# The order of two sums at the end of the first column: the half in the score banks ahead of the half in the value banks

## The chip, the cores and the metric

One core of one Trainium2 chip. The metric is the device time of one execution in microseconds, over several runs of each kernel. The changed kernel and the kernel before take turns on the same chip.

## The reference, cut to what matters

A gated attention unit feeds a gated feed-forward layer. Eight batches of 3008 rows, width 256, key width 64, hidden width 2048; inputs and output are float32.

```python
scores = scale * np.matmul(z, z.transpose(0, 2, 1))
attn = np.maximum(scores, 0.0) ** 2
out = np.matmul(attn, v)
attn_out = u * out
# ... as [24064, 256] = x into
h = x @ w_in
g = h * np.cos(h)
return (g @ w_out).astype(np.float32)
```

## The kernel before, where the change touches it

The attention is worked column by column (512 columns of the score matrix at a time). In the first three columns `phase_a_first` puts the value matmuls of both output halves beside the next scores. Each half takes two accumulators, one for the upper 64 rows and one for the lower 64, so four banks for a column: M0 and M1, and a pair E taken out of the rotation of three score pairs. A half is summed when the column ends:

```python
def gate_sum(s, b0, b1):
    W = width(s % NC)
    sm = spool.tile([P, CW], FP32, name="sm")
    nc.scalar.copy(sm[:, 0:W], b0[:, 0:W])
    nc.vector.tensor_tensor(sm[:, 0:W], b1[:, 0:W], sm[:, 0:W], ALU.add)
    return sm

def hold(src):
    nc.gpsimd.tensor_copy(mark[:, 0:1], src)

def phase_a_first(s, n, extra={}):
    # ...
    pair = [E[ea][:, 0, :], E[ea][:, 1, :]]
    acc = [pair, M] if s == 1 else [M, pair]
    # ... value matmuls and scores; within the loop, in later columns:
            if dh > 0 and (k % 4 == 3):
                drop_piece((b, J, k // 4))
                if s > 0:
                    emit_turns((0, 0), 1)      # one transpose of a piece A, on the SP queue
                    if k < 4:
                        turn_u(s)              # transpose of u, on the same queue
    # ... at the end of the column:
    late_sums.extend(gate_sum(s, *acc[dh]) for dh in range(2))
    hold(late_sums[0][0:1, 0:1])
    load_u(s + 1)
    e_order.append(ea)
```

`hold` is a one-element GpSimd copy that reads a sum. GpSimd works in order, so the load of the next u behind it isn't issued before that sum exists. The order of the calls:

```python
phase_a_first(0, 12, {4: lambda: turn_late(4), 8: lambda: turn_late(5)})
phase_a_first(1, 12)
nc.gpsimd.dma_start(w_out16, moe_w_out.rearrange("(k p) f -> p k f", p=P))
for i in range(2):
    emit_h(0, i)()
phase_a_first(2, 14)
# ...
phase_b(2)                                     # first use of w_out16
```

## Time and profile before

| | before |
|---|---|
| median of three runs | 1193.32 us (1192.68 to 1193.82) |
| span in the profile | 1191.2 us |
| TensorE busy | 1183.7 us, 99% |
| TensorE waits for the sum L278 | once, 0.7 us |

The lines are in the prediction below. A row of the timeline reads: start, duration, engine, line, operation, output<-inputs, shape, count, and in brackets the idle time ahead of it with what ended it. SPq is the queue of the DMA transposes. A transfer's landing is the moment at which its end is signalled. A row of the waits reads: who waited, for whom, total, times, longest.

On GpSimd, in the timeline of before: the hold and the load of u behind it, and the load of the output weights one column later.

```profile
24.49 0.18 POOL L353 CAST mark<-sm 1x1 f16<-1x1 f32 x1 [9.96 <-DVE sm L278]
24.72 0.57 POOL L148 DMA_DIRECT2D u<-in_u_dram  x1
...
39.09 1.18 POOL L721 DMA_DIRECT2D w_out<-in_moe_w_out_dram  x1
```

### The profile page before, as it was taken

To read this page: it belongs to the slowest core of one execution; us is meant where nothing else is said; L and a number is where in the kernel's file an instruction comes from. 1 tells how busy PE (TensorE), PEld (TensorE's weight loads), DVE (VectorE), ACT (ScalarE), POOL (GpSimd) and SP (SyncE) were. 2 spreads that over 40 slices of the span, in tenths; PEclk is the share of its full clock that TensorE was granted. 3 is DMA by queue.
4 is the path that set the end of the run, shared out by engine and by line. 5 is a ranking of instruction groups with operands and counts; after the bars stand their busy time and mean duration, and the time that the engine had idled before them with its cause. 6 is when DMAs were issued, how large, how long until landed. Compare 5 with 4: busy or idle time off the path is not lost.

```text
span 1191.2 us, 29044 instructions
## 1 busy us (share of the span) xinstructions
PE 1183.7 (99%) x11887; PEld 726.8 (61%) x11887; DVE 1011.5 (85%) x1302; ACT 794.9 (67%) x927; POOL 679.0 (57%) x717
## 2 busy tenths in 40 slices
PE   9999999999999999999999999999999999999998
PEld 4556665665566656666566665656666566665566
DVE  6888888889988898888988889888888888888776
ACT  7966676667666676667676676666766666666454
POOL 3286745657466573755647556476555655545452
PEclk9999999999999999999999999999999999999999
DMA  9999999569995799955999469984798837974301
GB/s 160 175 172 158 115 171 130 102 122 104 173 127 101 123 137 166 126 89 103 155 152 130 86 106 158 168 123 70 120 162 152 122 72 120 173 122 84 65 20 54
DMA packets 449142, 148.00 MB, mean 124 GB/s; under 512 B 401264, under 2 KB 432496, under 8 KB 449008
## 3 DMA queue, kind: packets, MB, share of 16 engines
q1 hardware_dynamic: 368464, 112.93, 56.6%
q0 software_dynamic: 80032, 32.78, 27.7%
q8 instruction: 93, 1.52, 0.5%
q10 hardware_dynamic: 512, 0.43, 0.1%
q14 instruction: 41, 0.34, 0.1%
HBM read 66.32 MB, written 24.64 MB: 76 GB/s over the span
## 4 chain that ended last, share of the span: by engine, by line
PE 98%; ACT 1%; DVE 1%; issue 0%; POOL 0%; DVEq 0%; ACTq 0%
PE E L412 27%; PE M L490 23%; PE M L266 20%; PE E L266 19%; PE E L202 6%; PE M L533 1%; ACT r L212 1%; PE M L468 1%; DVE g L423 0%; PE E L673 0%; DVE sm L278 0%; PE E L533 0%; POOL s L441 0%; PE M L696 0%; ACT c L420 0%
## 5 line engine op out<-in xcount | busy, mean ns | idle before, releaser
L420 ACT ACTIVATE c<-E 128x1024 f16<-128x1024 f32 (+1 forms) x384 | 385.7, 1007 | 216.4 <-PE E L412 214.1
L423 DVE SCALAR_TENSOR_TENSOR g<-E,c 128x1024 f16<-128x1024 f32 (+1 forms) x384 | 458.9, 1197 | 62.0 <-ACT c L420 60.9
L212 ACT ACTIVATE r<-E 128x512 f16<-128x512 f32 (+1 forms) x342 | 328.0, 967 | 112.3 <-PE E L202 106.6
L266 PEld LDWEIGHTS <-v 64*128 64x128 f16 x4512 | 245.7, 94 | 229.6 <-issue 18.8
L412 PE MATMUL E<-x,w_in 128*128 128x512 f16 (+1 forms) x1408 | 354.0, 375 | 0.0
L441 POOL TENSOR_TENSOR s<-g 128x512 f16<-128x512 f16 (+1 forms) x184 | 207.8, 1130 | 189.3 <-DVE g L423 139.4
L266 PE MATMUL M<-A,v 64*128 64x512 f16 (+1 forms) x2256 | 283.0, 372 | 0.0
L266 PE MATMUL E<-A,v 64*128 64x512 f16 (+1 forms) x2256 | 278.0, 371 | 0.0
L442 POOL TENSOR_TENSOR g<-g 128x512 f16<-128x512 f16 (+1 forms) x184 | 219.0, 1190 | 14.4
L412 PEld LDWEIGHTS <-w_in 128*128 128x128 f16 x1536 | 133.1, 98 | 108.9 <-issue 19.5
L490 PEld LDWEIGHTS <-g 128*128 128x128 f16 x2816 | 172.5, 98 | 40.8
L217 DVE TENSOR_TENSOR A<-r 128x1024 f16<-128x1024 f16 x240 | 173.2, 734 | 15.1 <-ACT r L212 14.3
L294 POOL TENSOR_TENSOR x<-sm,uT 128x512 f16<-128x512 f32 (+1 forms) x43 | 48.6, 1131 | 223.5 <-DVE sm L278 223.5
L490 PEld LDWEIGHTS <-s 128*128 128x128 f16 x2112 | 129.4, 98 | 32.1 <-DVE s L448 0.5
L202 PE MATMUL E<-zT 64*128 64x512 f16 (+4 forms) x684 | 128.0, 356 | 1.6 <-DVE sm L278 0.7
L448 DVE TENSOR_TENSOR s<-s,g 128x1024 f16<-128x1024 f16 (+1 forms) x92 | 99.7, 1085 | 2.1 <-POOL s L441 2.1
L490 PE MATMUL M<-w_mix,s 128*128 128x128 f16 x1408 | 94.0, 219 | 0.3 <-POOL s L441 0.3
L490 PE MATMUL M<-w_mix,g 128*128 128x128 f16 x1408 | 93.6, 219 | 0.0
L490 PE MATMUL M<-w_out,g 128*128 128x128 f16 x1408 | 93.6, 219 | 0.0
L220 DVE TENSOR_TENSOR A<-r 128x512 f16<-128x512 f16 (+1 forms) x102 | 80.1, 785 | 8.6 <-ACT r L212 7.6
L202 PEld LDWEIGHTS <-zT 64*128 64x128 f16 x684 | 38.7, 94 | 38.4 <-issue 3.8
L450 DVE TENSOR_TENSOR s<-g,s 128x1024 f16<-128x1024 f16 (+1 forms) x92 | 60.6, 661 | 0.0
(58 smaller groups left out, 636.3 us busy)
## 6 DMA issues: line engine op xcount, KB each, us to landing
out_dram<-o SPq DMA_DIRECT2D x87, 256.0 KB, 2.1
v<-in_v_dram POOLq DMA_DIRECT2D x40, 256.0 KB, 11.5
u<-in_u_dram POOLq DMA_DIRECT2D x40, 256.0 KB, 4.5
A<-A SPq DMA_TRANSPOSE x252, 5.3
z<-in_z_dram POOLq DMA_DIRECT2D x14, 192.0 KB, 10.9
z<-in_z_dram POOLq DMA_DIRECT2D x14, 176.0 KB, 6.8
v<-in_v_dram POOLq DMA_DIRECT2D x8, 192.0 KB, 16.1
u<-in_u_dram POOLq DMA_DIRECT2D x8, 192.0 KB, 3.7
```

Of the source, the lines that this page charges most:

```text
L202: nc.tensor.matmul(e[:, t, 0:Wt], zT[rows, k * P:(k + 1) * P], zT[rows, J * CW:J * CW + Wt], start=True, stop=True,)
L212: nc.scalar.activation(r[:, :, 0:W], e[:, :, 0:W], AF.Relu)
L217: nc.vector.tensor_tensor(a4, r4, r4, ALU.mult)
L220: nc.vector.tensor_tensor(a4, r[:, :, 0:W], r[:, :, 0:W], ALU.mult)
L266: nc.tensor.matmul(bank[:, 0:width(J)], vs[b, k // 4][t * H:(t + 1) * H, k % 4, dh * P:(dh + 1) * P], value_rhs(b, J, k, t), start=start, ...
L412: nc.tensor.matmul(e[:, f, 0:W], w_in16[:, k, ft * P:(ft + 1) * P], x[:, k, 0:W], start=(k == 0), stop=(k == 1),)
L420: nc.scalar.activation(c[:, :, 0:W], e[:, :, 0:W], AF.Sin, bias=half_pi, scale=inv_s2)
L423: return lambda: nc.vector.scalar_tensor_tensor(gs[m][:, 2 * i:2 * i + 2, 0:W], e[:, :, 0:W], 1.0, c[:, :, 0:W], ALU.mult, ALU.mult)
L441: nc.gpsimd.tensor_tensor(s1[:, f, 0:n], g[:, f, low], g[:, lower, low], ALU.add)
L442: nc.gpsimd.tensor_tensor(g[:, f, low], g[:, f, up], g[:, f, low], ALU.subtract)
L448: nc.vector.tensor_tensor(s2[:, f, 0:n], s1[:, f, 0:n], g[:, f, up], ALU.subtract)
L490: nc.tensor.matmul(acc[:, k * P:(k + 1) * P], left[:, ft, k * P:(k + 1) * P], right[:, ft, :], start=(ft == 0 and k == 0), stop=(ft == F - ...
```

## The change

Intent: release the score pair first, since a score needs it before any value matmul needs M.

```diff
         if s == 0:
             turn_u(0)
-        late_sums.extend(gate_sum(s, *acc[dh]) for dh in range(2))
+        sums = {dh: gate_sum(s, *acc[dh]) for dh in ((1, 0) if s == 0 else (0, 1))}
+        late_sums.extend(sums[dh] for dh in range(2))
         hold(late_sums[0][0:1, 0:1])
         load_u(s + 1)
         e_order.append(ea)
```

`hold` still reads the sum of the first half, which is now formed second.

## The prediction

> **What bounds the kernel now.** I read the page first, for the engine that sets the span, then that engine's waits, then the stretch where the longest of them stands. From the page:
>
> ```profile
> span 1191.2 us, 29044 instructions
> PE 1183.7 (99%) x11887; PEld 726.8 (61%) x11887; DVE 1011.5 (85%) x1302; ACT 794.9 (67%) x927; POOL 679.0 (57%) x717
> ...
> PE 98%; ACT 1%; DVE 1%; issue 0%; POOL 0%; DVEq 0%; ACTq 0%
> ```
>
> The TensorE is busy 1183.7 of 1191.2 us and carries 98% of the chain that ended last. All that it does not work is 1191.2 - 1183.7 = 7.5 us, and a change that leaves its matmuls alone can win only from there. Where that idle time lies is said by the waits of the TensorE, complete:
>
> ```profile
> PE E L673 <- DVE s L636: 1.2, 1, 1.2
> PE E L202 <- DVE sm L278: 0.7, 1, 0.7
> PE E L202 <- DVE g L423: 0.4, 1, 0.4
> PE M L490 <- POOL s L441: 0.3, 1, 0.3
> PE E L202 <- ACT zT L666: 0.3, 1, 0.3
> PE E L202 <- DVE zT L668: 0.2, 1, 0.2
> ```
>
> The second row is the one that the change aims at: once in the run, a score matmul (L202, into a pair of score banks E) waits for a sum (L278). The timeline from 22 to 26.5 us shows it:
>
> ```profile
> 22.52 0.38 PE L266 MATMUL M<-A,v 64*128 64x512 f16 x1
> 22.72 0.83 PE L266 MATMUL E<-A,v 64*128 64x512 f16 x6
> 22.99 0.58 ACT L277 COPY sm<-M 128x512 f32<-128x512 f32 x1
> 23.13 0.69 DVE L220 TENSOR_TENSOR A<-r 128x1024 f16<-128x1024 f16 x1 [0.34 <-ACT r L212]
> ...
> 23.46 0.60 ACT L277 COPY sm<-E 128x512 f32<-128x512 f32 x1
> 23.58 0.83 PE L266 MATMUL E<-A,v 64*128 64x512 f16 x6
> 23.74 0.68 DVE L278 TENSOR_TENSOR sm<-M,sm 128x512 f32<-128x512 f32 x1
> ...
> 24.34 0.68 DVE L278 TENSOR_TENSOR sm<-E,sm 128x512 f32<-128x512 f32 x1
> ...
> 25.07 0.39 PE L202 MATMUL E<-zT 64*128 64x512 f16 x2 [0.66 <-DVE sm L278]
> 25.29 0.61 PE L266 MATMUL E<-A,v 64*128 64x512 f16 x4
> 25.50 2.11 ACT L212 ACTIVATE r<-E 128x1024 f16<-128x1024 f32 x2 [0.51 <-PE E L202]
> 25.72 0.61 PE L266 MATMUL M<-A,v 64*128 64x512 f16 x4
> ```
>
> The first column has its first output half in the two banks M0 and M1 and its second half in a pair E. Each half is summed by a ScalarE copy (L277) of one bank and a VectorE addition (L278) of the other. M is summed first, though the E pair is what the next-but-one score needs; the matmul that reuses M comes later in the TensorE's order, at 25.72 us.
>
> **What the Trainium skill says.** "PSUM — Partial Sum Buffer", section on bank collisions, asks for semaphores by bank between engines, so the score may not touch the pair before the addition has read it; here the score starts 25.07 - (24.34 + 0.68) = 0.05 us after the addition's end, which agrees. The same page, "Engine vs sequencer instructions", says that matmuls start in program order; so the ready value matmuls behind the score wait too, and the trace shows none before 25.07. "TensorE: Matmul & The Clock Gate", "Back-to-back issue gap", gives about 216 ns for 512 columns; here 23.37 to 23.58 us from a score pair to the value pair behind it, 0.21, where two 64-row matmuls on different row halves go side by side. "Perfetto Trace Analysis", on the TensorE instruction, says that the ends are estimated; so I count from starts, not from the 0.66.
>
> **The change, part by part.** The order of instructions of both builds was compared. No instruction is added or removed. On ScalarE the two copies swap, on VectorE the two additions swap, the rest keeps its place. Two first matmuls of the second column into M0 and M1 get an explicit wait (for the copy of M0, for the addition of M1). Nothing in the other 1160 us differs.
>
> 1. Copy of E: ScalarE is free for it at 22.99 (it follows the last relu of the column). The pair's last value matmul started with that of M0 at 22.52; results reach ScalarE about 0.43 us after a start (25.07 to 25.50), thus 22.95. It fits by 0.04, so the copy begins at 22.99 and ends near 23.58.
> 2. Addition of E: it takes the place of the first addition, at 23.74, behind the square of 23.13, and ends at 23.74 + 0.68 = 24.42.
> 3. Score: 24.42 + 0.05 = 24.47 in place of 25.07, a gain of 0.60 us. Without any wait it would go three pairs after 23.58, at 23.58 + 3 x 0.216 = 24.23. So the wait is 25.07 - 24.23 = 0.84 now and 0.24 after: the change takes 0.60 of it and leaves 0.24 (0.06 by the profile's way of counting idle time).
> 4. M: its addition now comes second, 24.34 to 25.02, and with 0.05 frees M1 at 25.07. The first value matmul into M stands 25.72 - 25.07 = 0.65 behind the score, so at 24.47 + 0.65 = 25.12. It fits by 0.05 us.
> 5. Behind it: from 25.07 to 36.4 the scores start at steps of 0.86 or 1.08 us, four or five pairs of 0.216, so there the TensorE never waits and ScalarE follows it. ScalarE ends its earlier relu near 24.99 and can take the next from about 24.9, when the score's result is there. So the whole column moves 0.6 us earlier.
> 6. The 0.4 us wait of 39.88 us (score for L423) hangs on the last relu of the second column, its copies, additions and two L423: all follow ScalarE and so the TensorE, and move along. The wait stays 0.4 and eats nothing.
>
> The chain of waits of before confirms that the two additions lie on the path here and the TensorE after them:
>
> ```profile
> 23.13 0.69 DVE A L220
> 23.82 1.21 DVE sm L278 x2
> 25.03 0.04 issue
> 25.07 0.39 PE E L202 x2
> 25.46 0.43 PE E L266 x4
> ```
>
> One addition less on it is 1.21 / 2 = 0.60, the same by a second way. No wait of the TensorE after 45 us is longer than 0.3, so 0.60 us should arrive at the end: 1193.32 - 0.6 = 1192.7 us.
>
> **Rivals.**
> (a) The wait moves to M: the addition that frees M1 ends 0.05 us before it is needed. If signals come 0.1 us later than I take them, the TensorE stops at 25.12 instead for about that long. For it: the margin is as small as what I can read from the timeline. Against: even if M made it wait as long as E did, no more than the 0.60 could go. It would make 1192.8, at worst 1193.3.
> (b) A later load takes it back. The load of the next u is held back until the sum of the first half is formed (a small POOL copy, 24.49), and that sum moves from 24.42 to 25.02. The transpose of this u starts at 29.16 as it lands, and five transposes of A follow it on the same queue to 49.3 us; all may come 0.6 us later while the TensorE comes 0.6 us earlier. Against: the first three columns compute their own score pieces and wait for no transposed piece. The transposed u of this slot is first used at 45.86, some 13 us after its landing; the source pieces are overwritten from 48.9 us on, those of the transposes of 39.03 and before. The output weights, issued at 39.09 and 14.4 us to landing (53.49), are used at 54.62: 1.1 us of slack for load and transposes to push each other about. It would make 1193.0 to 1193.5.
> (c) The wait at 39.88 swallows the gain, if VectorE does not come earlier there. It would make 1193.3. Against: step 6; VectorE's squares before it all wait for ScalarE (0.22 to 0.39 us each).
> (d) The run-to-run spread hides everything: the three runs of before lie between 1192.68 and 1193.82, 1.14 us, twice the effect. This I hold to be certain for single runs; it does not change the middle.
>
> **Range and chances.** The whole idle time of the TensorE is 7.5 us, 0.6% of the time, and 2% would be 23.9 us: faster by over 2% cannot come from this change, and nothing that it moves could cost so much short of a disturbed run. So within 2% gets 0.99. The middle is 1192.7. The gain itself I put between 0 and 0.7 us; with half the spread of the runs on either side the range is 1192.0 to 1193.5.
>
> **What would show it.** Right: the copy of E at 22.99 and its addition at 23.74; the score at 24.47 with hardly any idle before it; in the waits of the TensorE, the 0.7 for the sum gone or 0.1; the first M matmul of the second column near 25.12; the wait of 0.4 still there, near 39.3 us; the TensorE's busy time still 1183.7 and the span near 1190.6; VectorE's idle before its second square of the column falling from 0.84 to about 0.3; the transpose of u at 29.8. Step 1 is wrong if the copy of E starts late, step 4 if a wait of M matmuls (L266) for the sum appears, step 6 if the wait for L423 grows towards 1 us, rival (b) if the TensorE waits for a DMA anywhere. The prediction as a whole is wrong if the same rounds on one chip show the changed kernel slower, or faster by over 1 us.

## The result and the profile after

| | before | after |
|---|---|---|
| median | 1194.12 us (1192.68 to 1197.46, 6 runs) | 1196.70 us (1195.15 to 1197.47, 6 runs) |
| ratio of the fast runs | 1 | 1.0015 (1.0000 to 1.0031) |
| span in the profile | 1191.2 us | 1193.5 us |
| TensorE busy in the profile | 1183.7 us | 1183.3 us |
| TensorE waits for the sum | 0.7 us | none |
| TensorE waits for the output weights | none | 2.9 us |

A ratio is the mean time of one kernel's fast runs over that of the other's in the same rounds, so it isn't quite the ratio of the medians. By the 2% threshold this is "same", but its middle is a loss (the interval just touches 1), and the prediction had a gain of 0.6 us. A second set of rounds (below, the changed kernel again) gave 1.0022, with 1 outside the interval.

The page of after, and the TensorE's waits:

```profile
span 1193.5 us, 29044 instructions
...
PE 1183.3 (99%) x11887; PEld 726.7 (61%) x11887; DVE 1010.9 (85%) x1302; ACT 794.2 (67%) x927; POOL 679.3 (57%) x717
```

```profile
PE M L534 <- DMA w_out<-in_moe_w_out_dram: 2.9, 1, 2.9
PE E L674 <- DVE s L637: 1.2, 1, 1.2
...
PE E L202 <- DVE g L424: 0.4, 1, 0.4
```

The wait for the sum is gone and a new one leads the list. Its size fits the span: 2.90 new less 0.66 removed is 2.24 us, and the span grew by 1193.5 - 1191.2 = 2.3. So nothing else of size happened, and the place to look is one transfer.

The timeline of after around the swapped sums:

```profile
22.75 0.58 ACT L277 COPY sm<-E 128x512 f32<-128x512 f32 x1
...
23.34 0.83 PE L266 MATMUL E<-A,v 64*128 64x512 f16 x6
23.49 0.68 DVE L278 TENSOR_TENSOR sm<-E,sm 128x512 f32<-128x512 f32 x1
...
24.09 0.68 DVE L278 TENSOR_TENSOR sm<-M,sm 128x512 f32<-128x512 f32 x1
24.23 0.39 PE L202 MATMUL E<-zT 64*128 64x512 f16 x2
...
24.78 0.69 DVE L217 TENSOR_TENSOR A<-r 128x1024 f16<-128x1024 f16 x1
24.84 0.68 POOL L353 CAST mark<-sm 1x1 f16<-1x1 f32 x1 [11.34 <-DVE sm L278]
24.87 0.61 PE L266 MATMUL M<-A,v 64*128 64x512 f16 x4
...
25.46 0.57 POOL L148 DMA_DIRECT2D u<-in_u_dram  x1
```

This execution is 0.24 us early as a whole (its value matmuls ahead of the wait start at 23.34, in before at 23.58). With that taken off, the score starts at 24.23 + 0.24 = 24.47, as predicted. The hold's copy is the row to look at: it took 0.68 us in place of 0.18, and the load behind it was issued at 25.46, just as the square of 24.78 ended (24.78 + 0.69 = 25.47). The load of u was issued 25.46 + 0.24 - 24.72 = 0.98 us later than in before, not 0.60.

From the same timeline, one column later, the load of the output weights, VectorE held by a transpose of A, and the TensorE where it lost the time:

```profile
38.24 1.17 POOL L722 DMA_DIRECT2D w_out<-in_moe_w_out_dram  x1
...
52.65 1.29 DVE L217 TENSOR_TENSOR A<-r 128x1024 f16<-128x1024 f16 x2 [1.47 <-DMA A<-A]
...
56.84 1.05 PE L534 MATMUL M<-w_out,g 128*128 128x256 f16 x8 [2.90 <-DMA w_out<-in_moe_w_out_dram]
```

The load was issued 0.85 us earlier than in before (38.24 against 39.09) and landed 3.3 us later. The view of the tile of the output weights gives the time to landing, in before and then in after:

```profile
DMA to landing us min/median/max: 14.4/14.4/14.4
```

```profile
DMA to landing us min/median/max: 18.5/18.5/18.5
```

39.09 + 14.4 = 53.5 us against 38.24 + 18.5 = 56.7 us. What slowed it is on the transposes' queue. Its timeline in before, and then in after (start, duration of the issue, count):

```profile
29.16 1.94 SPq L168 DMA_TRANSPOSE uT<-u  x1
31.19 18.10 SPq L252 DMA_TRANSPOSE A<-A  x5
49.38 4.04 SPq L168 DMA_TRANSPOSE uT<-u  x1
```

```profile
29.33 1.49 SPq L168 DMA_TRANSPOSE uT<-u  x1
30.91 21.64 SPq L252 DMA_TRANSPOSE A<-A  x5
52.65 3.98 SPq L168 DMA_TRANSPOSE uT<-u  x1
```

The five transposes of A took 3.5 us longer too. So both transfers are slower while they run side by side.

### The profile page after: what moved, and what is told of

Its sections match the earlier page's. It is cut to its first block, busy times and chain, and to the rows that moved or that the text cites. A ratio compares the mean times of both kernels' runs of the same rounds, so it can differ in the third digit from the quotient of the medians.

```text
span 1193.5 us, 29044 instructions
## 1 busy us (share of the span) xinstructions
PE 1183.3 (99%) x11887; PEld 726.7 (61%) x11887; DVE 1010.9 (85%) x1302; ACT 794.2 (67%) x927; POOL 679.3 (57%) x717
## 4 chain that ended last, share of the span: by engine, by line
PE 95%; DMA 2%; issue 1%; ACT 1%; DVE 0%; POOL 0%; ACTq 0%; POOLq 0%
PE E L413 27%; PE M L491 23%; PE M L266 20%; PE E L266 18%; PE E L202 5%; DMA w_out<-in_moe_w_out_dram 2%; PE M L534 1%; ACT r L212 1%; PE M L469 1%; PE E L674 0%; PE E L534 0%; DVE g L424 0%; DVE sm L278 0%; POOL s L442 0%; POOL u L148 0%
## 5 line engine op out<-in xcount | busy, mean ns | idle before, releaser
L443 POOL TENSOR_TENSOR g<-g 128x512 f16<-128x512 f16 (+1 forms) x184 | 219.3, 1192 | 14.4
```

Of the source, the lines that this page charges most:

```text
L443: nc.gpsimd.tensor_tensor(g[:, f, low], g[:, f, up], g[:, f, low], ALU.subtract)
```

## The experiments

**The theories.** A: the change itself makes the output weights late each time, by shifting transfers against each other. A1: the later hold alone does it. A2: it takes the later hold and the earlier TensorE together. B: the landing is chance, alike in both kernels. Twelve kernels were run, five rounds each, in three groups of four; the kernel before ran nine times in each group. The second group (runs 5 to 8) ran on another chip than the other two.

**1. The kernel before once more** (no edit).

> The kernel before, unchanged, for a second trace. Theory A (the reordered sum moves the load of the output weights into the transposes, each time): the output weights land ahead of their first use as in the first trace of before, the TensorE waits 0.7 us for the sum and not at all for that load, ratio to before 1.000. Rival B (the load's landing is chance from run to run, in both kernels alike): a wait of 1 to 3 us for the output weights may stand here too, and the 6 timed runs of before, 1192.7 to 1197.5, are this spread.

Measured: 1193.08 us against 1193.16, ratio 0.9999 (0.9987 to 1.0012). The waits are those of the first trace: the sum 0.7, no load. The weights needed 15.8 us from 38.87 and thus landed at 54.7. The TensorE's timeline of this trace, and then of the first one:

```profile
52.66 1.90 PE L412 MATMUL E<-x,w_in 128*128 128x512 f16 x8
54.67 1.05 PE L533 MATMUL M<-w_out,g 128*128 128x256 f16 x8
```

```profile
52.88 1.90 PE L412 MATMUL E<-x,w_in 128*128 128x512 f16 x8
54.62 1.04 PE L533 MATMUL M<-w_out,g 128*128 128x256 f16 x8
```

From the start of the eight matmuls to the first use of the weights it is 2.01 us here and 1.74 in the first trace. So the TensorE did wait 0.27 us for the weights; the list of waits hides it, as it counts from the estimated ends. The kernel before had no slack at all in this execution, where the first trace had shown 1.1 us.

**2. The changed kernel once more** (no edit).

> The changed kernel, unchanged, for a second trace. Theory A: again a wait of 2 to 3.5 us of the TensorE for the output weights, no wait for the sum, ratio 1.0015 to 1.002. Rival B: the wait may be absent or of another length, and the ratio over more rounds falls to 0.9995 to 1.001.

Measured: 1196.29 us (1194.24 to 1197.95) against 1193.16, ratio 1.0022 (1.0009 to 1.0034). Its waits:

```profile
PE M L534 <- DMA w_out<-in_moe_w_out_dram: 1.0, 1, 1.0
...
PE M L534 <- DVE sm L278: 0.3, 1, 0.3
```

The wait is there again. The profiled execution was the quickest of the five (1194.24), which fits 1.0 in place of 2.9. The size falls short of what theory A had said for the trace; the loss over the rounds is just above the 1.0015 to 1.002 that it had said. B is out as the cause of the loss: two sets of rounds show it, and of two traces each the changed kernel has waits of 1.0 and 2.9 us and the kernel before none and 0.27. But the landing does vary from run to run.

**3. The output weights one column earlier, in the changed kernel.**

```diff
+    nc.gpsimd.dma_start(w_out16, moe_w_out.rearrange("(k p) f -> p k f", p=P))
     phase_a_first(1, 12)
-    nc.gpsimd.dma_start(w_out16, moe_w_out.rearrange("(k p) f -> p k f", p=P))
     for i in range(2):
```

> The changed kernel with the load of the output weights issued one column earlier (ahead of the second column, behind the load of the next u) instead of behind the second. Both theories expect the wait for the output weights gone. Theory A: the gain of the reordered sum then shows, TensorE idle 2.3 to 3 us less than in the changed kernel, ratio to before 0.9990 to 0.9998; a small wait may be left, since the sum of the second column on VectorE came late as well, behind a square that waited 1.5 us for a transpose. If the ratio stays at 1.0015, the load was not what cost the time.

Measured: 1192.58 us (1192.28 to 1193.04) against 1193.16, ratio 0.9993 (0.9981 to 1.0006), span 1190.6, no wait for a load and none for the sum. The load of the weights is where the time was lost; without it the span is the 1190.6 us that was predicted, though the interval of the ratio includes 1.

**4. The hold on the sum that is formed first, in the changed kernel.**

```diff
-        hold(late_sums[0][0:1, 0:1])
+        hold(sums[1 if s == 0 else 0][0:1, 0:1])
```

> The changed kernel, but the small GpSimd copy that holds back the next load of u waits for the sum that is now formed first (of the second half), so the load isn't 0.6 us later. Theory A1 (the transposes are late because the load of u and its transpose were held back by the later sum): the transpose queue runs 0.5 to 0.6 us earlier, the wait for the output weights falls under 1 us, ratio 0.9995 to 1.0005. Theory A2 (the load of the output weights starts 0.9 us sooner with the TensorE and so meets a whole transpose that it trailed before): the wait stays at 2 to 3 us, ratio 1.001 to 1.002.

Measured: 1192.57 us (1192.42 to 1193.09) against 1193.16, ratio 0.9994 (0.9980 to 1.0007), span 1190.8. The hold's copy is short again, and the weights, issued only 0.35 us later than in the changed kernel, land in 13.7 us (52.3). From the timeline of this kernel, GpSimd:

```profile
24.49 0.18 POOL L353 CAST mark<-sm 1x1 f16<-1x1 f32 x1 [9.96 <-DVE sm L278]
24.72 0.57 POOL L148 DMA_DIRECT2D u<-in_u_dram  x1
...
38.59 1.18 POOL L722 DMA_DIRECT2D w_out<-in_moe_w_out_dram  x1
```

The theory A2 for this run, that the earlier load of the weights alone is enough, is out: the earlier TensorE alone costs nothing, and in the changed kernel the later hold is necessary for the loss.

**5. The later hold alone, in the kernel before.**

```diff
-        hold(late_sums[0][0:1, 0:1])
+        hold(late_sums[1 if s == 0 else 0][0:1, 0:1])
```

> The kernel before, sums in the old order, but the small GpSimd copy that holds back the next load of u reads the second sum in place of the first; nothing else. Theory A1 (the later hold alone is what costs): the copy stands at about 25.1 us, takes 0.68 instead of 0.18 us behind a VectorE square, the load of u starts about 1.1 us later than in before, the TensorE keeps its 0.7 us wait for the sum and gets a wait of 0.5 to 3 us for the output weights; ratio 1.001 to 1.003. Theory A2 (the reordered additions and the earlier TensorE are needed for the loss): ratio 0.9995 to 1.0005.

Measured: 1193.05 us against 1193.30, ratio 0.9997 (0.9984 to 1.0010), no wait for the weights. The copy was long and the load of u late as expected:

```profile
25.03 0.68 POOL L353 CAST mark<-sm 1x1 f16<-1x1 f32 x1 [11.48 <-DVE sm L278]
25.66 0.57 POOL L148 DMA_DIRECT2D u<-in_u_dram  x1
```

The expectation from A1 failed: a hold that delays the load of u by 0.94 us (25.66 against 24.72) costs nothing by itself either. A2 holds at this delay: it takes both. Run 10 asks what a longer delay does.

**6. The control for 3: the weights one column earlier, in the kernel before.** The edit is that of 3.

> The kernel before with the load of the output weights one column earlier, the control for the same edit of the changed kernel. Theory A1: in before this load was in time, so nothing is won: ratio 0.9995 to 1.0005, and the same edit of the changed kernel (0.9993) is then 0.0005 better by the reordered sum alone. If the ratio here is 0.9993 too, the gain of that run came from the earlier load and not from the sum.

Measured: 1193.01 us (1192.91 to 1193.42) against 1193.30, ratio 0.9994 (0.9980 to 1.0007). It keeps its 0.7 us for the sum and has the span of before, 1191.2. The ratio lies a hair under what was expected, drawn by one run of before at 1197.06; the medians differ by 0.3 us. Its span against that of run 3, 1191.2 to 1190.6, differs by the reordered sum alone: 0.6 us, in one profiled execution each.

**7. The transpose of u two places later in its queue, in the changed kernel.** The late load of u stays late, but the transposes of A no longer stand behind it.

```diff
-                    if k < 4:
+                    if k // 4 == (2 if s == 1 else 0):
                         turn_u(s)
-                    elif k < 8:
+                    elif k // 4 == 1:
```

> The changed kernel with the transpose of the held-back u put two places later in the transposes' queue, behind the first two transposes of A of the second column; the load of u stays as late as the change made it. If the transposes of A are late because they queue behind that of u (head of the line), they start at 27 to 29 us instead of 30.9, the wait for the output weights goes, ratio 0.9990 to 0.9998. If the late load itself disturbs (its own packets), the wait stays and the ratio is 1.001 to 1.002.

Measured: 1192.65 us (1191.89 to 1193.10) against 1193.30, ratio 0.9990 (0.9977 to 1.0002). The first transpose of A behind the hold starts at 28.5 us. A wait of 0.6 us for the weights was left in the trace, so the expectation that it goes was met in part; over the rounds the loss is gone (the medians differ by 0.65 us; the 1197.06 of before helps this ratio too). So the late load acts, at least for the greater part, through the transposes that queue behind its own.

**8. A delay of 0.5 us ahead of the load of u, in the kernel before.**

```diff
         hold(late_sums[0][0:1, 0:1])
+        if s == 0:
+            nc.gpsimd.memset(xodd[:, 0, :], 0.0)
         load_u(s + 1)
```

> The kernel before with a GpSimd memset of 512 columns between the hold and the load of u, which delays that load by about 0.5 us and changes nothing else: the size of the delay that the prediction had reckoned with (0.6), without the 0.5 us that the hold's copy lost behind a square. If 0.5 us is enough, a wait for the output weights of 0.3 us or more appears and the ratio is over 1.0005; if it takes the whole 1.1 us, ratio 0.9996 to 1.0004 and no such wait.

Measured: 1193.33 us against 1193.30, ratio 0.9998 (0.9986 to 1.0011), no wait for the weights. The memset began under the copy's end, so the load came 0.36 us later (25.08 against 24.72), not 0.5. This agrees with 5 and says nothing more than it: without the earlier TensorE, neither delay is enough.

**9. The weights issued 1 us later, in the changed kernel.**

```diff
+    nc.gpsimd.memset(xodd.rearrange("p a b -> p (a b)")[:, 0:1024], 0.0)
     nc.gpsimd.dma_start(w_out16, moe_w_out.rearrange("(k p) f -> p k f", p=P))
```

> The changed kernel with a GpSimd memset of 1024 columns (about 1 us) between the third load of u and the load of the output weights, so that this load is issued later than in the changed kernel, about 13.8 us behind the second load of u in place of 12.8 (it was 13.5 to 14.4 in all runs without the loss). Collision theory (the weights' packets must not reach the DMA engines before those of the transpose of A that lies ahead of them): issued 1 us later they begin at 43.5 to 44.5 instead of 42.4, land earlier, at 51.5 to 54, and the wait falls from 1.0 to 2.9 us to 0.6 or less; ratio 0.9985 to 0.9998. Rival (the load simply has too little time): the wait grows by 1 us, ratio 1.002 to 1.004.

Measured: 1193.09 us (1192.49 to 1193.32) against 1193.45, ratio 0.9996 (0.9982 to 1.0009), span 1190.9, no wait for the weights. GpSimd in its timeline, and the time to landing:

```profile
38.76 0.97 POOL L722 MEMSET xodd<- 128x1024 f16 x1
39.65 1.17 POOL L723 DMA_DIRECT2D w_out<-in_moe_w_out_dram  x1
```

```profile
DMA to landing us min/median/max: 13.6/13.6/13.6
```

A load that was issued 1.4 us later than in the changed kernel landed at 39.65 + 13.6 = 53.3, which is 3.5 us earlier. So too little time was not the trouble. The first packet came at 45.0 us, later than the 43.5 to 44.5 expected.

**10. The same distance of the two loads, in the kernel before:** the edit of 5, with a memset of 768 columns behind the hold.

> The kernel before, old order of the sums, hold on the second sum and a GpSimd memset of 768 columns (about 0.75 us) behind it: the second load of u is issued about 1.8 us later than in before, 12.7 us ahead of the load of the output weights, the same distance as in the changed kernel, but the TensorE isn't earlier. Collision theory (the distance of the two loads decides): the weights' packets begin near 42.5 to 43.3, more than 650 KB of transposes run beside them, they land at 55 to 57, wait 0.5 to 2.5 us, ratio 1.0005 to 1.002. If the earlier TensorE is needed, no wait and ratio 1.000.

Measured: 1194.02 us (1193.73 to 1197.97) against 1193.45, ratio 1.0014 (1.0000 to 1.0027), and in the trace

```profile
PE M L535 <- DMA w_out<-in_moe_w_out_dram: 0.2, 1, 0.2
```

The ratio grew as expected, by two runs of five (1196.31 and 1197.97; the other three lie between 1193.73 and 1194.02), and the wait appeared. But in the profiled execution it was 0.2 us (0.39 counted by starts as in run 1) in place of 0.5 to 2.5, and the weights' first packet came at 44.3 us, not 43.3 or before. The distance of the two issues (12.8 us, as in the changed kernel) isn't the whole rule. And with a load of u that is 1.66 us late (26.38 against 24.72) the loss seems to come without an earlier TensorE, so "it takes both" holds for the 0.94 us of run 5 only.

**11. A delay of 0.5 us in place of the hold's long copy, in the changed kernel:** the edit of 4, with a memset of 512 columns behind the hold. 

> The changed kernel with the hold on the sum formed first and a GpSimd memset of 512 columns (0.52 us) behind it: the load of u is then as late against the TensorE as the prediction had reckoned (0.6 us), without the 0.5 us that the hold's copy loses behind the VectorE square in the changed kernel; distance of the two loads about 13.35 us. If that 0.5 us tipped it: no wait over 0.6 us for the output weights, ratio 0.9990 to 0.9998. If 0.6 us was enough already: wait 1 to 3 us, ratio 1.001 to 1.002.

Measured: 1192.86 us (1192.41 to 1195.48) against 1193.45, ratio 0.9998 (0.9985 to 1.0010), span 1190.6, no wait for the weights. As in run 8 the memset delayed the load by 0.36 us only, counted from the hold's start (24.86 - 24.27 against 24.72 - 24.49), so this isn't quite the 0.6 us that was meant. With the TensorE early, 0.36 us of delay shows no loss in four of the five runs (the fifth took 1195.48 and wasn't profiled), and 0.98 us does. Whether the 0.60 us that the prediction had reckoned with would have been enough is open.

**12. The best of it:** the edits of 3 and 4 together.

> The best version that the runs point to: the sums in the new order, the hold on the sum formed first, and the load of the output weights one column earlier. No wait for the sum or for a load; TensorE idle as in the other two repaired versions, ratio 0.9990 to 0.9997, not better than either of them by more than 0.0003.

Measured: 1192.31 us (1192.26 to 1192.55) against 1193.45, ratio 0.9990 (0.9978 to 1.0003). All five runs lie under all nine of before (1192.78 to 1194.78), though the interval touches 1. It also has the smallest spread of all, 0.3 us. Its lead over run 4, 0.0004 against the 0.0003 at most that was expected, is far inside the intervals.

**What the packets say.** The trace keeps every DMA packet with its queue, start and size. The output weights travel as 2048 packets of 512 bytes on the software queue, a transpose of a piece A as 2048 packets of 256 bytes on the hardware queue. The fifth transpose of the column (that of u counted, so the fourth of A) is the one that the weights meet. Counted from the packet records (us from the span's start; "u ends" is the start of its last packet, "landing" the issue plus the time to landing, "wait" what the list of waits has, so that the 0.27 us of run 1 doesn't appear):

```
run                     u ends  weights: issue  first  landing   transpose ahead: packets before   its last   wait   ratio
                                                  packet           the weights' first packet      packet
after (first trace)      42.6        38.24      42.4   56.7                  111                    51.3      2.9   1.0015
changed kernel again     42.9        38.49      42.5   55.1                   45                    52.5      1.0   1.0022
10 hold second, pad      43.2        39.18      44.3   55.0                 1226                    47.8      0.2   1.0014
7 u's transpose later    42.5        38.28      43.5   54.5                 1296                    47.5      0.6   0.9990
5 hold second            43.3        39.13      44.2   54.3                 1088                    48.1       -    0.9997
1 before again           42.9        38.87      44.3   54.7                 1621                    46.6       -    0.9999
before (first trace)     43.0        39.09      44.4   53.5                 1689                    46.1       -    1
8 pad                    42.7        39.09      44.2   53.9                 1659                    45.9       -    0.9998
9 weights later          43.3        39.65      45.0   53.3                 1992                    47.8       -    0.9996
11 hold first, pad       42.1        38.37      43.7   52.2                 1850                    44.5       -    0.9998
4 hold first             42.2        38.59      44.0   52.3                 1997                    44.2       -    0.9994
```

In all kernels the third load of u, just ahead of the weights on the same queue, ends at 42 to 43.3 us. The transpose of A begins before that (first packet at 40.3 to 42.4), but only 108 to 469 of its packets have passed when u ends. In the kernels without loss 1088 packets or more of the transpose pass before the weights' first, and it is done by 44 to 48 us. In the two traces of the changed kernel the weights' first packet comes 4.0 to 4.2 us after its issue (elsewhere 5.1 to 5.4), while u's last packets still pass, and only 45 and 111 packets of the transpose have passed. From then on the two queues alternate: in the second trace of the changed kernel between 47 and 48 us there were 240 packets of the weights and 239 of the transpose, where each alone ran at some 390 and over 1100 a us (run 4). The transpose of A then lasts until 51 to 52 us, the next one starts behind it, and all the time it is beside the weights. "DMA: Bandwidth & Descriptors" of the Trainium skill, section "Queues, rings and completion order", says that a DMA engine goes round its queues packet by packet. A packet of that page holds several descriptors, and the trace doesn't show how long one turn is; but the 240 against 239 agree with even turns.

Why the order turns round is argued from these rows, not shown by a run of its own. The weights' packets seem ready about 4.1 us after their issue, and that issue comes 0.52 us after that of the third load of u. So they can follow u at once if u takes about 4.6 us or more to end. It took 4.9 us in both traces of the changed kernel (issued at 37.73 and 37.97) and 4.1 to 4.5 us in before and in runs 1, 4, 8 and 11. The difference lies ahead of its first packet, which came 2.1 us after the issue in the changed kernel and 1.4 to 1.5 us after it in those others. In nine of the eleven traces this packet stands 0.02 to 0.14 us behind the last one of the fourth transpose of the column (in runs 7 and 9 0.3 to 0.4 us ahead of it), so it is likely the late transposes that hold u up. Runs 5, 7 and 10 lie between, with 4.6 to 4.7, and so do their packet counts. Run 9 has 5.1, but 0.9 us more between the issues.

**Open.** Where the single slow runs of before come from (1197.46, 1197.06) isn't known: none was profiled. That the three kernels with the weights a column earlier (runs 3, 6 and 12) never passed 1193.42 in fifteen runs suggests the same near miss, and shows no more than that. Run 10 was slower over five rounds than its profiled execution explains. So was the changed kernel: its two traces account for 2.3 and 1.1 us of span, its medians for 2.6 and 3.1 us. In its first rounds two runs took 1195.15 and 1195.24 us at a listed clock of 1.000, and four took 1196.47 to 1197.47 at 0.998; in the second, 1196.91 and 1197.95 are at 0.998 too, as is the 1197.97 of run 10, and no other run whose clock is on record lists less than 0.999. None of these seven was profiled, so it isn't shown whether they waited longer for the weights or lost time to the clock. In all kept traces the lower clock stands only after the last matmul.

## Why the prediction was wrong

- Steps 1 to 3, the copy, the addition and the score: right to 0.01 us. Score at 24.47 after the shift of 0.24, and 24.23 - (23.34 + 3 x 0.216) = 0.24 us left of the wait, as worked out.
- Step 4, M in time: right. The first M matmul came 0.64 us behind the score, no wait for M.
- Step 5, the column follows: right. VectorE's idle time before the second square fell from 0.84 to 0.24 us (about 0.3 was expected).
- Step 6, the 0.4 us for L423 moves along: right, at 39.03 (39.27 with the shift).
- The end, "0.60 us should arrive at the end": wrong. Runs 3, 4 and 11 have spans of 1190.6 to 1190.8, so it arrives when the transfers are left in their order. In the changed kernel it met the new wait of 1.0 and 2.9 us.
- **The step that failed is the case against rival (b)**, as the prediction put it: "1.1 us of slack for load and transposes to push each other about". Three terms of it were mis-sized. The slack came from one trace, in which the landing took 14.4 us; the same kernel took 15.8 in the next. The delay of the load of u was put at 0.6 us, and was 0.98, because the hold's copy ran behind a square and let the load go 0.38 us later still. And "push each other about" was taken for a small continuous effect, while the order of two transfers turned round (the packet counts show it, why is argued only): the time to landing rose to 16.6 and 18.5 us.
- The "source pieces" of (b) were mis-sized likewise: VectorE waited 1.47 us for a transpose of A before it could overwrite one, and in the second trace 2.4 us, of which 0.3 us reached the TensorE through the sum.
- "It would make 1193.0 to 1193.5" was too mild: the medians are 1196.70 and 1196.29 against 1194.12 and 1193.16. The rival was named and the rest of the chain was right, but it was given too little weight, and the range ended below the outcome. Its upper end doesn't follow from its own recipe either: no gain and half the spread is 1193.32 + 0.57 = 1193.9, not 1193.5. The outcome lies beyond both.
- Rival (d): single runs do overlap (before reached 1197.46), as it said, but the middle moved, which it excluded.

The hold could have been read from the page of before and a page of the skill: "SBUF — State Buffer", section "Who interferes with whom", says that a VectorE instruction with two SBUF inputs contends with a GpSimd instruction that reads SBUF. The square r x r is such an instruction, the addition of the sum with one operand in PSUM is not; in before the copy ran beside the addition, in after behind the square: 0.18 against 0.68 us.

## What to carry to other kernels

When a sum moves, look for everything that reads it, also what reads it only to be late: here a one-element copy paced a load, the load a transpose, and that transpose a queue. A kernel tuned to 99% on one engine may owe its quiet to the order in which transfers happen to meet, so read the slack of a landing from several executions, and issue a load that a whole phase needs well ahead instead of just in time (run 12 has the lowest median and the smallest spread, though its lead over runs 3 and 4 isn't clear of noise). If an earlier issue lands later, look at what it overtook.

## What the Trainium skill lacked or had wrong

- "DMA: Bandwidth & Descriptors" states the packet-by-packet turns; the runs put a cost to them: two transfers of 2048 packets, of 512 and 256 bytes, ran at 240 packets a us each side by side, against some 390 and over 1100 alone, and the landings of the first came 13.6 to 18.5 us after the issue.
- The same page gives one time to the first byte on the software queue, and no page read here says what becomes of it behind another load: here the output weights' first packet came 4.0 to 4.2 us after the issue where it followed that load's at once, 5.1 to 5.4 us where a transpose had come in between.
- "TensorE: Matmul & The Clock Gate", section "Back-to-back issue gap", gives some 131 ns a matmul of 512 columns for a stream with weight loads; the eight 128-row matmuls of L412, each with its weight load, take 1.90 us on end in before, of which one takes 0.38, thus (1.90 - 0.38) / 7 = 0.217 us each. That is its figure for a single matmul, about 216 ns, the one that the prediction used.
- "SBUF — State Buffer" agrees (0.18 against 0.68 us); that such a stall of one element can set the time of a transfer is for the kernel's author to see.
